# A written-out order of 3,900 entries replaced: other queue orders, one early subtraction moved from GpSimd to VectorE, 13 more products of zeros

## Chip, cores and metric

The kernel runs on one core of a Trainium2 chip. The metric is the device time of one execution in microseconds (us); the time of a kernel is the median of its runs. Three runs of the kernel before gave 851.04, 850.16 and 851.88 us, so their median is 851.04 us.

## What is computed

Attention with two kinds of windows, and behind it two layers of the same shape, all in float32 to the accuracy of float32:

```
scores = q @ k.T / sqrt(64)            # 4 batches, 8 heads, 576 positions, head size 64
mask: heads 0-3: 0 <= i-j < 32;  heads 4-7: 0 <= i-j < 128 and (i-j) % 4 == 0
x = softmax(scores) @ v                # as 2304 tokens x 512
h = x @ w_in;  x = relu(h)**2 @ w_out          # layer 1, 512 -> 2048 -> 512
h = x @ w_in2; out = (h * sigmoid(h)) @ w_out2 # layer 2, same shapes
```

The weights come in as 64-bit floats and are turned into pairs of 32-bit floats on the chip.

## The kernel before

**Products in three parts.** TensorE multiplies in the type fp32r, which keeps fewer bits than float32. So every operand is split in a high part (a cast) and a low part (the subtraction `x - high`, `Kern.sub`, profile line L252), and every product is three matmuls: high x high, high x low, low x high. Casts are at L245 (ScalarE) or L247 (VectorE), and the splits load VectorE most.

**Stages.** Attention works on 32 blocks: half a sequence (288 positions, index h from 0 to 7) times a pair of heads (0 to 3). A block's scores are matmuls at L525. VectorE adds the mask and takes the row minimum (L550). For the first four blocks (h = 0) the method `late_exp` follows: `less` subtracts the row's value from the scores (L683 on VectorE, L686 on GpSimd; one call for each of the two heads of the pair), TensorE transposes the result (L705), ScalarE takes the exponential (L721), TensorE multiplies by the values and a column of ones (L730), VectorE adds a small constant to the row sums (L736) and inverts them (L738), ScalarE or VectorE scales (L746, L743), and TensorE turns the block round (L622). The later blocks do the same in another order (L558 to L622).

Layer 1 begins while attention goes on: `mlp` runs the first three tiles of 256 tokens (L780 to L782 for the first product, L828 to L830 for the second), `mlp2` three tiles of 512 tokens (L928, L982 to L984), and layer 2, `strassen`, three tiles of 768 tokens with seven products in place of eight (L1086, L1171). `weights` loads one piece of the weights as 64-bit numbers (L274), turns it into 32-bit ones (a scaling at L282 on ScalarE or L284 on VectorE, a shift at L293 on VectorE or at L295 on GpSimd, bit operations at L302, L305 and L309), splits it, and writes some of it back to DRAM (L340 and others); `stream` loads such pieces again when a tile needs them (L437).

**Order by hand.** No compiler sets the order. `Planner.order` reads the string `ORDER`, 3,900 entries, and issues the operations in that sequence. An entry is a letter, the number of the operation, and after each `@` the place of a buffer that it takes. The letter names the engine: P TensorE, V VectorE, A ScalarE, G GpSimd, D a transfer, and F a bundle of products of zeros on TensorE (`filler`, L1237), of which the number is the count. Each engine runs its own entries in the order of the string and waits for the operands of the first one that isn't ready. All transfers are issued by one queue, SyncE's (SP), in the same way: a transfer waits until the buffer that it writes is free, or the data that it stores are made, and whatever is behind it waits too. Places count from 0 to about 205 in units of 256 columns of one large on-chip region; two operations that use the same place follow one another.

A GpSimd entry also waits for the last marked VectorE entry before it in the string (`o.turn`, L137, and L1305 to L1308).

**Entries that matter here.** P5 and P36 are the scores of blocks 0 and 1 of h = 0; P67 and P98 those of blocks 2 and 3. V9 and entry 20 are the subtractions for the two heads of block 0 (`less`), V40 and V51 those of block 1, V72 and V83 of block 2, V114 and V103 of block 3. P10 and P21 transpose block 0's two heads, P41 and P52 block 1's. A11, A12, A22 and A23 are block 0's exponentials. P13, P24, P44 and P55 are the products with the values of blocks 0 and 1, P28, P59, P90 and P121 turn blocks 0 to 3 round. D2, D33, D64 and D95 load the queries and keys of the four blocks, D126 and D134 the first two pieces of weights; A127 or V127 scales D126's piece, G128 is its `shift` in GpSimd's form (L295). P1202 is the first product of layer 1. D2283 loads the 256 KB of `w1s` (tile `wc`) that the fourth group of products of step 6 of layer 1's fifth tile needs (P2398). V1753 or A1753 makes the high part of one piece of `w2`, entry 1754 its low part, and D1755 writes the high part and the low part back (`w2s`).

Of the kernel before, what the change touches and what calls it, by code (L numbers as in the profile page):

```python
# [1360 lines left out]
A172@195 V160 A161@100 V1206 D474@26 V166 V167 A1210 A1211@130 P475@3@1@138@2 V489 P1207 V162 P1214@2 V476
A154@168 A477 V491 A492 V480 V478 A479 V173 V493 V168 D261@40 D194@124 V1212 A481 V482 V155 A494 A490 A169@172
P394@1@0@7@0 V397 V495 P387@3 A390@104 A388 V395 P1213 V496 A1215@122 A1216 A1217@118 V483 A485 V404 V396 P398@1
A498 G181 V405 V389 V406 P407@2 V174 V497 V391 V182 V1218 V170 A399 P400@3 A484 A408 P409@2 P486@0 V401 V175
V410 D186@153 A187@5 G188 P499@1 A195@16 V196 A488 P1219 A501 A487 A500 P502@0 D209@187 A210@191 A176@120 V411
V402 V403@183 V183 V412 P413@1 D201@149 V177 P1220@2 V189 A505@146 A503 V504 V190 D507@52 A414 A416 V415
A184@176 V185 D224@108 D418@89 D239@194 D506 A1221@181 A1222 A1223@116 P508@0@3@74@2 V509 A510 V511 A191@28 V524
V513 F7@2 V1224 P1225 V202@202 V417 V522 A512 A514 V197 A523 A525 V526 V198 A527 V528 V515 V192 V529 A530 A531
V516 A517 A518 V203 V199@180 P420@3@0@94@1 V432 V433 V434 V421 V422 P1226@1 P532@2 A534 A1227@161 A1228 V431
P435@0 V204 V423 V424 P425@1 P519@3 A225@199 A436 A262@2 A533 V419 P437@0 A426 P427@1 A520 A521 P535@3 V211 V212  # L1370
V226 V205 V200 V428 A1229@18 V1230 P1231 V438 A206@32 G207 V213 D216@153 A217@95 D231@10 V429 V439 V430@7 V440
A538@132 A536 V537 V227 V218 A214@184 P441@2 A240@78 A232@141 A442 V443 V219 A444@52 V445 V220 V215 P1238@1
A1239@158 A1240 A1241@24 V1242 F5@0 A221@88 G222 D148 D540@127 P541@3@0@149@2 V544 V555 V548 V559 A556 D178
D254@113 D133 D291@80 D446@144 P448@1@2@136@0 V451 A560 V557 A558 A549 V449 V542 V561 A562 V546 P1243 D193 V450
V233 A547 V452 P453@3 A543 A545 A454 V563 V461 V564 P1250@0 V459 V228 V550 V460 V447 V234 V551 V462 P463@3 V552
A229@188 V230 V565 A1251@56 A1252 P455@2 V456 A464 A1253@92 V1254 V457 P553@1 A554 P465@3 V466 V235 D246@73
V458@124 P566@0 V467 P1255 V241 V263 V242 A255@24 V256 A567 P568@0 A468 A236@96 V237 A569 P469@1 A470 V471
A247@12 A571@26 P1232@3 A1233@147 V243 A244@192 A472 A1234 A1235@5 V248 V570 V257 V249 V473 P1262@2 A1263@141
A1264 A1265@108 P1244@0 A1245@37 A1246 A1247@199 D573@15 P574@2@1@20@1 V245 V264 V250 A251@128 V590 V579 V575
A591 V581 V594 A595 V577 V592 V588 A589 D208 D606@7 D284@152 A593 A576 A578 G1248 D276@160 P1256@3 V265 V1515@56  # L1380
P607@2@0@36@0 V610 V621 V1236 V619 V612 P1268@1 P1237 P1249 V1266 V252 V258 A1257@156 A580 A620 V623 A582 V596
A611 A1269@144 V583 V584 V597 V1514@117 V1516@124 V608 P1280@0 A1258 D539 D269@197 V585 P586@2 V1517 V598
V1526@12 A285@0 A622 A1259@72 A1270 A277@110 A1271@146 A624 V625 A266@40 V278 V286 V279 V1260 A613 A609 A1520
A587 V1518@112 P599@1 V614 V1519 V287 V267 V615 P1274@3 A1275@158 P1267 A600 P601@2 A1276 A1523 A270@92 P1261
D633@201 A602 A604@108 D605 D572 D163 D238 V626 V288 A627 A616 V1524 P1286@3 V280 A1287@150 V603 V1272 V1521
P628@2 A629 A1281@4 P617@1 A1288 P1273 A618 A292@140 A1277@147 V271 V272 A281@72 V273 A274@136 V1282 V293
P634@3@1@76@3 V635 V637 V639 A640 V646 V648 V259@132 V650 D299@56 D660@196 D1525 D1522 V260 V282 P630@0
A1289@117 A631@22 V1278 A636 A638 V641 V642 V275 V643 P1292@2 A1293@108 A1294 P1298@3@0@1 A1283@24 A1299@153
A1300 V1527@155 V294 V1290 V295 V1284 P1304@2 V1530@36 A1305@142 P644@3 A645 A1306 A649 P1279 P661@3@2@16@0
V1539@20 P1291 G1528@116 A300@80 A1307@14 V668 V675 A651 V289@144 A647 V652 A676 A1295@157 V653 A654 V664 V666  # L1390
V677 V662 V679 V681 V296@68 P1285 V1538@162 V1296 P655@3 V1540@24 A669 A663 A656 A665 V1529 V297 A667 V670 V1531
D306@92 A678 A682 V671 V301 V1308 V672 V290 A1301@159 A1532 V1302 P1310@2 A1311@148 P1316@3 A1317@150 A1535
A1318 A1319@7 A1312 A1313@82 A680 D223 P1297 V302 V1541 V683 V1542@84 V1543 V1320 P657@3 A307@157 V308 P673@2
A674 V684 A658@4 A685 P1303 V1536 V1550@12 V1314 V303 V309 P1322@2 P1309 D321@112 D632 D314@124 A1323@76
D691@201 A1324 A304@140 V315@162 V305 D329@108 D1537 A1325@58 V322@152 V1533 D1534 P686@3 A687 A1547 V1548 V310
V323 V1551@14 V1326 P1328@2 A1329@78 A1330 A1331@10 P1334@3 A1335@100 A1336 A1337@102 P688@2 A689@16 A1544
A311@116 V316 V317 V318 P1315 P692@3@2@0@2 V695 V710 A696 P1321 V693 A694 V706 V699 A700 V697 A698 A711 A707
V708 A709 V712 A713 P1346@2 V701 V702 V703 P704@3 A705 V1332 V1545 V714 V715 A1347@20 A1348 D722@196 V312
V1562@154 P1327 A716 V319@148 P723@3@2@76@1 V728 A729 V724 A725 V726 A727 V737 V1338 V739 A740 A1349@38 V741
D298 D1546 D690 D1549 D268 D659 D351@92 P1333 V730 V1563@9 V1350 V731 V324 P1340@3 A738 V733 A742 P717@2 A718  # L1400
# [261 lines left out]
```

## Time and profile before

| | us |
|---|---|
| median of 3 runs | 851.04 |
| lowest, highest run | 850.16, 851.88 |
| the profiled execution | 854.73 |
| its span, first to last instruction | 853.0 |

| engine | busy us | share of the span | instructions |
|---|---|---|---|
| TensorE (PE) | 841.8 | 99% | 6012 |
| VectorE (DVE) | 667.9 | 78% | 1786 |
| ScalarE (ACT) | 472.9 | 55% | 1268 |
| GpSimd (POOL) | 35.5 | 4% | 43 |

The profiled execution is a run of its own, 3.7 us above the median of the timed ones; its instructions lie in a span that is 1.7 us shorter than its time. A matmul's end is modelled and matmuls overlap, so that TensorE counts as busy through short waits inside a group of products; the distance from start to start shows those. The page's chain of work that ended last is on TensorE for 90% of the span.

### The profile page before, as it was taken

How to read it: one execution, taken by the hardware profiler on the slowest of the kernel's cores; microseconds unless marked ns; L12 is line 12 of the kernel's file. 1: busy time of each engine (PE TensorE's matmuls, PEld its weight loads, DVE VectorE, ACT ScalarE, POOL GpSimd, SP SyncE). 2: the span in 40 equal slices, each digit the busy share in tenths (PEclk: the TensorE clock that was granted, in tenths of full speed). 3: DMA queues.
4: the chain of work that ended last, by engine and by line, in shares of the span. 5: the costliest groups of instructions: out<-in, count | busy, mean ns of one | idle time of the engine just before them, and what ended most of it. 6: DMA issues, size and time to landing. Idle time of an engine off the chain costs nothing.

```text
span 853.0 us, 16835 instructions
## 1 busy us (share of the span) xinstructions
PE 841.8 (99%) x6012; PEld 797.1 (93%) x6012; DVE 667.9 (78%) x1786; ACT 472.9 (55%) x1268; POOL 35.5 (4%) x43
## 2 busy tenths in 40 slices
PE   8999999999999999999999999999999999999998
PEld 6889999999989989988889899999999999999998
DVE  5999999989987898788899996789812598524782
ACT  3898988767565435333323546675334674346740
POOL 2110000000110000000000000100000000000000
PEclk7999999999999999999999999999999999999999
DMA  7774666778997898976999999886883464965642
GB/s 285 253 259 169 195 231 220 257 246 290 352 318 282 295 337 276 325 289 221 361 317 376 353 325 354 309 281 219 293 316 140 159 237 153 333 207 206 215 155 75
DMA packets 83603, 223.56 MB, mean 262 GB/s; under 512 B 8768, under 2 KB 18240, under 8 KB 83520
## 3 DMA queue, kind: packets, MB, share of 16 engines
q1 hardware_dynamic: 83520, 222.49, 74.4%
q8 instruction: 48, 0.79, 0.4%
q14 instruction: 35, 0.29, 0.1%
HBM read 172.13 MB, written 50.33 MB: 261 GB/s over the span
## 4 chain that ended last, share of the span: by engine, by line
PE 90%; DMA 4%; DVE 4%; ACT 1%; issue 1%; SPq 0%; POOL 0%; DVEq 0%; ACTq 0%
PE y L1086 17%; PE s L928 14%; PE sa L1171 14%; PE y L1171 6%; PE y L982 5%; PE y L983 5%; PE y L984 5%; PE sa L1086 4%; PE s L780 2%; PE ax L525 2%; PE s L782 2%; PE s L781 2%; PE ax L617 1%; PE y L828 1%; PE y L830 1%; PE ax L594 1%
## 5 line engine op out<-in xcount | busy, mean ns | idle before, releaser
L252 DVE TENSOR_TENSOR hl<-gq,hl 128x384 fp32r<-128x384 f32 x164 | 86.4, 562 | 31.9 <-ACT hl L245 31.5
L1086 PE MATMUL y<-xs,ws 128*128 128x384 f32 x552 | 107.0, 334 | 0.0
L245 ACT CAST hl<-gq 128x384 fp32r<-128x384 f32 x168 | 77.4, 512 | 51.1 <-DVE gq L252 20.3
L1086 PEld LDWEIGHTS y<-xs,ws 128*128 128x128 f32 x552 | 96.6, 188 | 0.1
L1062 ACT COPY gq<-y 128x384 f32<-128x384 f32 x92 | 43.1, 480 | 76.6 <-PE y L1086 73.2
L1171 PE MATMUL sa<-hl,wp 128*128 128x384 f32 x432 | 78.6, 334 | 0.0
L928 PE MATMUL s<-x,ws 128*128 128x256 f32 x576 | 76.9, 284 | 0.0
L982 PE MATMUL y<-g,w 128*128 128x512 f32 x192 | 76.2, 397 | 0.0
L1171 PEld LDWEIGHTS sa<-hl,wp 128*128 128x128 f32 x432 | 75.2, 188 | 0.0
L983 PE MATMUL y<-g,w 128*128 128x512 f32 x192 | 75.2, 392 | 0.0
L984 PE MATMUL y<-g,w 128*128 128x512 f32 x192 | 74.8, 390 | 0.0
L558 ACT ACTIVATE ap<-ap,ast 96x128 f32<-96x128 f32 (+3 forms) x168 | 62.3, 372 | 21.5 <-DVE ast L550 18.7
L928 PEld LDWEIGHTS s<-x,ws 128*128 128x128 f32 x576 | 72.8, 191 | 1.3
L944 DVE TENSOR_TENSOR h<-s,h 128x512 f32<-128x512 f32 x96 | 59.6, 621 | 15.4 <-PE s L928 11.2
L1057 DVE TENSOR_TENSOR gq<-y,gq 128x384 f32<-128x384 f32 x46 | 25.0, 553 | 57.4 <-PE y L1086 46.7
L245 ACT CAST g<-r 128x256 fp32r<-128x256 f32 (+1 forms) x94 | 47.7, 508 | 35.1 <-DVE r L964 16.3
L780 PE MATMUL s<-x,w 128*128 128x256 f32 x192 | 56.4, 294 | 0.1
L782 PE MATMUL s<-x,w 128*128 128x256 f32 x192 | 54.5, 284 | 0.1
L781 PE MATMUL s<-x,w 128*128 128x256 f32 x192 | 54.3, 283 | 0.1
L252 DVE TENSOR_TENSOR g<-r,g 128x256 fp32r<-128x256 f32 (+1 forms) x91 | 49.5, 548 | 4.8 <-ACT g L245 4.4
L252 DVE TENSOR_TENSOR gq<-gq 128x384 f32<-128x384 f32 x95 | 50.3, 552 | 3.7 <-ACT gq L1122 3.2
L1171 PE MATMUL sa<-hl,sw 128*128 128x384 f32 x288 | 51.4, 335 | 0.1
(157 smaller groups left out, 1972.4 us busy)
## 6 DMA issues: line engine op xcount, KB each, us to landing
raw<-w SPq DMA_DIRECT2D x64, 512.0 KB, 6.1
ws<-w1x SPq DMA_DIRECT2D x48, 512.0 KB, 6.5
ws<-w2x SPq DMA_DIRECT2D x48, 512.0 KB, 6.3
sw<-w2y SPq DMA_DIRECT2D x48, 512.0 KB, 4.8
wa<-w1s SPq DMA_DIRECT2D x24, 512.0 KB, 5.4
wa<-w2s SPq DMA_DIRECT2D x24, 512.0 KB, 6.5
w1x<-st SPq DMA_DIRECT2D x16, 512.0 KB, 3.7
w2x<-st SPq DMA_DIRECT2D x16, 512.0 KB, 5.9
```

What stands on the lines that cost most here:

```text
L245: self.nc.scalar.copy(out=out, in_=in_)
L252: self.eng[eng].tensor_tensor(out=out, in0=a, in1=b, op=ALU.subtract)
L558: es.append(self.op({"ACT": c_act(nk) + 0.185}, lambda e, i=i, n=n, c=c, p=p, st=st: nc.scalar.activation(out=p.tile[:n, c], in_=p.tile[:n ...
L780: nc.tensor.matmul(o, wh.tile[:, s], xh, start=(kk == 0), stop=False)
L781: nc.tensor.matmul(o, wh.tile[:, s], xl, start=False, stop=False)
L782: nc.tensor.matmul(o, wl.tile[:, s], xh, start=False, stop=(kk == KC - 1))
L928: nc.tensor.matmul(bank.tile[:, o:o + 256], wp, xp, start=i == 0, stop=last, skip_group_check=True)
L982: nc.tensor.matmul(o, wh.tile[:, s], gh.tile, start=c == 0, stop=False)
L983: nc.tensor.matmul(o, wh.tile[:, s], gl.tile, start=False, stop=False)
L984: nc.tensor.matmul(o, wl.tile[:, s], gh.tile, start=False, stop=(c == NF - 1))
L1086: nc.tensor.matmul(o, w[part == 2].tile[:, kk * P:kk * P + P], x[b][part == 1].tile[:, kk * half:kk * half + half], start=new and not kk a ...
L1171: nc.tensor.matmul(o, u.tile[:, c * P:c * P + P], v.tile, start=new and not q and not part, stop=q == nf - 1 and part == 2, skip_group_che ...
```

## The change

The diff replaces `ORDER` as a whole: 245 lines go, 246 come, and no other line changes. Both strings hold the same 3,892 operations and eight bundles of zeros, each operation once. What differs:

- The order on each engine. Of TensorE's 746 entries 297 have another rank among TensorE's, by at most 14; of VectorE's some 1,400 of 1,560, by at most 41; of ScalarE's some 930 of 1,035, by at most 31; of the 516 transfers 469, by at most 21.
- The engine of 141 operations, nearly all of them casts, copies and scalings that change between VectorE and ScalarE. Entry 20, the subtraction of block 0's second head, goes from GpSimd (L686) to VectorE (L683). Entry 127 goes from VectorE to ScalarE, entry 1754 from VectorE to GpSimd, and 1753 from ScalarE to VectorE.
- The buffers' places (851 operations).
- The bundles of zeros: 10, 9, 4, 7, 8, 6, 7, 5 (56 in all) become 14, 11, 7, 7, 12, 8, 5, 5 (69).

The beginning of the string, and the lines around D2283, 1754 and D1755, before and after:

```diff
@@ -1348,250 +1348,251 @@
 APART = ()
 V_LAG = 3
 ORDER = """
-V1 F10@0 D2@72 P5@22@0 G0 V17 V6 V19 V18 D33@67 V7 P36@112@1 V8 V9 V37 V48 F9@1 P10@0 G20 P21@1 A11 V39 A22 V50
-V49 V51 P52@2 A53 A12 A23 A54 D64@195 P67@58@2 D126@173 V127@55 G128 V38 V40 P41@2 A43 A42 D34@100 V80 D96@90
-D3@43 V4 F4@0 D134@145 A135@9 D95@165 V71 V68 V129 V70 P13@0 V14 V35 V79 V15 P24@1 V25 V81 V69 V26 V82 A16@155
-A27 P44@3 V45 V46 A47@77 V72 P98@72@3 V100 V101 V112 V113 P55@2 V56 V57 D65@64 F7@0 P73@0 V102 A58 A74 V66 V99
-V83 V111 V110 V114 P28@1 A31@48 A29@44 V32 V136 V30 P59@2 A62 P84@3 A85 P75@0 V76 V103 A60 V61 V97 V77 V63
-P115@3 A116 P86@1 V87 V78@170 D141@122 A142@82 P104@3 A105 D366@15 F8@3 V88 A89 P90@3 A91@60 A93@64 V137 V130
-A131@68 G132 V138 V143 A139@164 G140 D149@107 A150@88 V92 P106@0 V107 V94 P117@2 V118 V108 V119 V109@182 V120
-P368@3@1@1@0 V369 V378 V379 F6@0 D392@133 D156@36 A157@31 A3890 D164@111 V380 P381@2 A382 V371 V370 V144 V367
...
-V2385 P2381@2 D2288@60 D2237 D1747 P2343 D2283@14 D1766@201 V1767@32 V1768 D2284@39 P2395@0 P2396@1 A1760 V2355
-V1754 A2392@196 V2393 V2402 V2403 V2404@110 V2246@108 V2387@10 A2247@44 V2249@34 V2248 V1770 D2289@39 A2388@201
-P2429 P2430 A1843@16 V1844 V1845 V1779@60 V1780 V1787 P2431 A1819@42 G1820 D1755 A1826@18 V1827 V1821 V2500
...
+V1 F14@1 D2@166 P5@140@3 G0 V8 V7 V6 V18 V9 D33@79 P36@33@1 V17 D126@89 A127@157 G128 F11@3 P10@3 A11 V19 V20
+P21@0 A22 A12 A23 V37 V50 V48 V39 V38 V40 D64@151 P67@186@2 P41@2 A42 D3@99 V4 P13@1 V49 V51 P52@0 A53 A54 A43
+D34@0 D134@29 A135@104 V68 V79 V70 V129 V80 V35 V82 V14 V15 V69 F7@3 P24@0 V71 V72 V81 P44@3 V45 V25 V26 V46
+A16@130 V27 P55@2 V56 V83 V57 A47@20 A58 V136 D95@174 P98@201@0 V111 V102 V112 V113 V110 D65@119 V66 V101 V100
+V114 P73@0 P28@1 A29@44 A74 A31@48 V30 F7@3 P59@2 A60 V61 P84@3 A85 A62 V32 P75@0 V76 V99 P115@3 A116 P86@1 V77
+A78@71 V103 P104@3 A105 V87 V63 V88 A89 F12@2 D179@7 D96@110 V97 D141@146 A142@170 P90@3 A91@60 A93@64 V130
+A131@68 P106@0 V137 V138 A139@164 D156@23 A3890 A157@34 V143 V92 V107 P117@2 V118 V94 V108 V109@120 V119 V120
+D366@79 P368@3@1@1@3 V379 V380 V378 G132 F8@0 G140 V369 V371 V370 P121@1 A122 V144 A180@192 A124 V367 V158
+D149@153 D164@18 D261@40 A150@11 P381@0 A382 P372@3 A373 V145 A146@84 A165@36 V123 P1202@2 V151 V159 A1203@146
...
+V2370@94 A2371@42 V1185 P1199@0 V2374@12 A2375@197 V2383 V2384 V1753@120 G1754 D1170 D1766@20 D2287@78 D1729
+P2397@1 P2360 D2236@96 D2238@28 D1201 V2387@26 V2376 V2391@32 D2237 D1755 A2240@48 D2283@24 P2398@0 P2373 D2239
...
 """
```

## Rows read from the trace of the kernel before

**Rows 1.** Windows: us, then busy us (instructions) of each engine, clock, DMA share, GB/s

```profile
0.00:27.28 27.28, 22.78 (x188) 18.25 (x189) 16.23 (x100) 11.88 (x40) 5.04 (x15) 0.81 0.83 298
27.28:100.00 72.72, 71.55 (x726) 66.58 (x726) 71.52 (x288) 64.53 (x212) 7.22 (x7) 1.00 0.59 202
100.00:140.00 40.00, 39.93 (x389) 38.11 (x387) 38.62 (x141) 35.45 (x123) 0.74 (x1) 1.00 0.71 245
140.00:380.00 240.00, 238.68 (x1995) 219.28 (x1992) 208.19 (x632) 135.54 (x449) 8.82 (x8) 1.00 0.84 294
380.00:849.40 469.40, 468.77 (x2726) 454.88 (x2724) 333.30 (x629) 224.98 (x446) 13.71 (x13) 1.00 0.73 256
```

**Rows 2.** Timeline of TensorE, first 10 us: start us, us, line, operation, tiles

```profile
0.98 2.31 PE L1237 MATMUL fill<-warm 128*128 128x256 bf16 x10 [0.98 <-DVE warm L1229]
3.75 2.66 PE L525 MATMUL y<-w 64*96 64x96 f32 x24 [0.46 <-DMA w<-qkv]
6.35 1.16 PE L1237 MATMUL fill<-warm 128*128 128x256 bf16 x9
7.35 0.44 PE L705 MATMUL ax<-ident,ap 96*128 96x96 f32 x3
8.86 0.30 PE L705 MATMUL ax<-ident,ap 96*128 96x96 f32 x1 [1.06 <-POOL ap L686]
9.71 1.06 PE L705 MATMUL ax<-ident,ap 96*128 96x96 f32 x5 [0.56 <-POOL ap L686]
```

**Rows 3.** Waits of TensorE, the longest in total: us, times, longest

```profile
PE ax L705 <- POOL ap L686: 1.6, 2, 1.1
```

**Rows 4.** Windows around the stretch at the lower clock, columns as in rows 1

```profile
6.28:9.70 3.42, 1.81 (x15) 1.21 (x13) 3.42 (x22) 1.53 (x2) 2.39 (x4) 1.00 1.02 376
9.70:19.93 10.23, 10.16 (x74) 8.57 (x75) 5.65 (x44) 4.76 (x20) 0.59 (x1) 0.50 0.76 302
19.93:40.00 20.07, 18.67 (x193) 16.58 (x191) 18.80 (x79) 16.30 (x52) 2.51 (x2) 1.00 0.76 256
```

**Rows 5.** Timeline of VectorE, 5 to 11 us

```profile
5.42 0.25 DVE L550 CUSTOM_DVE_ANT_0 ap<-y,mask 96x96 f32<-96x96 f32 x1 [4.49 <-PE y L525]
...
6.62 0.58 DVE L683 TENSOR_TENSOR ap<-ap,ast 96x96 f32<-96x96 f32 x2
...
8.12 0.60 DVE L683 TENSOR_TENSOR ap<-ap,ast 96x96 f32<-96x96 f32 x2
...
9.21 1.52 DVE L683 TENSOR_TENSOR ap<-ap,ast 96x96 f32<-96x96 f32 x2
```

**Rows 6.** Timeline of GpSimd, 7 to 11 us

```profile
7.31 2.35 POOL L686 TENSOR_SCALAR ap<-ap,ast 96x96 f32<-96x96 f32 x3 [4.84 <-DVE ap L683]
9.64 0.65 POOL L295 TENSOR_SCALAR raw<-raw 128x512 f32<-128x512 f32 x1
```

**Rows 7.** Groups of VectorE's instructions by form: count, busy us, mean ns

```profile
L284 DVE TENSOR_SCALAR cv<-raw 128x512 f32<-128x512 f32 x23 | 9.7, 420 | 2.3 <-DMA raw<-w 2.3
L247 DVE CAST st<-cv 128x512 fp32r<-128x512 f32 x10 | 4.2, 420 | 0.5 <-issue 0.4
```

**Rows 8.** Around a load near 385 us: SP, landing, entry 1754, TensorE, GpSimd's splits, write-back

```profile
364.35 0.37 SPq L437 DMA_DIRECT2D wc<-w1s  x1
...
wc<-w1s SPq DMA_DIRECT2D x1, 256.0 KB, 7.6
...
384.07 0.69 DVE L252 TENSOR_TENSOR st<-cv,st 128x512 fp32r<-128x512 f32 x1
...
386.39 0.88 PE L928 MATMUL s<-x,wc 128*128 128x256 f32 x6
...
L252 POOL TENSOR_TENSOR st<-st 128x512 fp32r<-128x512 f32 x2 | 2.6, 1294 | 33.3 <-DMA ws<-w2x 33.3
...
405.82 0.43 SPq L340 DMA_DIRECT2D w2s<-st  x1
```

More of the change, by code (lines that the diff above doesn't have):

```diff
@@ L1361 @@
[L1361 to L1400, printed above, removed]
@@ new lines @@
+V1041 P2122 A2137@108 V2138 V1039 A2133@47 V2134 A1000 A1009 D1670@93 D2069@21 D1696@6 D2071@106 A1029 A1013
+A1011 A1027 A1042 V1014 V1015 V1032 A1033 V1034 V1035 V1671@26 V1017 V1001 V1002 A1697@14 V1045 V1672 A1040
+V1036 A1004 A1046 P2140@3 P2141@0 P2135 P2139 A2144@49 V1016 V2145 V1691 D961 D2072@28 D1509 D2079@98 A1003
+V1673 V1674 V1678@108 P1005@3 A1007 P1018@0 P1037@1 D1507 D2075@10 D930 V1680@92 D2070@54 D1055@196 D1669
+P2142@2 A1044 V1047 V1020 D2074@76 A1019 A1006 P1021@3 D2073@44 V1048 D992 V1049 P1050@0 A1038 V1022@58 V2146
@@ new lines @@
+V1095 V2216 V2217@73 V1105 V1106 A1107 D1085 D2033 P2173 P2186 P2190 D1714@97 P1108@2 D1684 D2034@49 D2035
+D1722@108 D1703 V1709 D1710 D2258@33 V1715@13 V1716 V2206 V1096 V2042@85 V2045@57 P1097@1 P2203 P2207 D1687
+D2261@9 V2048@31 V1115 V1130 D2262@112 V1126 D2260@45 D2266@22 A2218@40 V2219 A1098 A1116 A1127 A1118 A2046@116
+V1119 V2221@37 A1120 V1717 V1109 V1718 A2038@64 V2039 V2051@75 V1128 A2040@80 A2222@71 A2052@88 V1719@27
+A2036@104 A1131 A1129 V1723@68 V2041 V1724 V2037 P1110@3 V2053 D1740@96 V1121 V1122 V2223 A1123 P2220 P2224
@@ new lines @@
+D2472@108 P2428 P2429 P2515@1 P2430 P2516@0 P2517@3 A2432@14 P2431 V1821 V1822 V1826@18 V1827 V1828 V1790
+V2503@4 D2471@88 V1829 A1823@203 V2510@97 D1791 V2519 V2520 V1832@60 G1824 V2521 D2477@128 V1834@198 V2522
+V2527@57 V1833 V2436@122 P2531@0 P2532@1 A2535@32 V2523@30 V2536 D1866@72 D2474@84 A1867@0 V1868 V2434@90
+A2524@23 A2438@2 A2504@124 P2533@2 P2534@3 P2548@1 V1835 A1839 V2505 P2506 P2507 D1792@92 V1793@8 P2508
+A2511@117 V2512 P2509 P2513 V2537 V1869 D1773 V1846 V2538 V2539 V2540@88 D2476@40 V2525 P2526 D2481@4 D1849@100
@@ new lines @@
+D2478@96 V2544@27 D1890@64 D1873@10 D2475@80 D2437 D2433 D2484@32 V1840 D1841 A1836 V1837 A2528@68 V1870
+V1850@124 V1851 V1852 V2529 D2480@20 D2483@14 D2439 D2479@29 D1838 V1794 A2541@116 P2549@3 P2550@2 P2551@0
+A2552@172 V2553 V2542 P2530 V2554 V2555 V2556 V2561@80 V2557@110 V1795 V1853 V1856@164 V1796 V1857 V1858@198
+V1859 P2565@1 A2569@82 P2566@2 P2567@1 D2482@168 V2570 V2571 V1874@70 V2572 A2558@174 V2559 V1875 A1863 A2545@60
+V2546 A1860 P2568@0 P2543 P2547 D2487@68 V1876 V1877 V1861 A2562@40 V1864 P2582@3 P2583@2 D2485@120 P2584@1
@@ new lines @@
+D1897@92 A1898@102 G1899 A1891@100 V1892 D1865 P2560 V1882@116 V2573 V1880@72 V1881 V2574@2 A2575@32 V1893 V1900
+A1884 A2586@23 V2587 V2563 V2588 V2589 V2578@182 V1871@178 G1872 P2585@3 V2590 V2595@126 V1901 D2486@108
+V2591@80 A2592@24 V1883 V2576 V1894 A2579@120 V2580 V1904@28 P2599@1 A2603@168 A1797@4 D2435 D1862 D1914@86
+D2491@57 D2488@96 D2489@196 P2564 P2600@2 P2601@1 P2602@0 V1906@108 V2604 V2605 V2606 V1798 A1847@197 V1885
+V1905 V2607 V2612@91 V1848 V1907 V2608@128 P2577 D2490@10 P2616@3 A2620@189 D2492@82 P2617@2 D2440@172 D2441
@@ new lines @@
+D2713@56 P2991 P2995 V2998 A3037@72 A3029@60 V3048 V3030 P3002@0@3 A3041@42 A3045@119 D2644@66 D3087@161
+D3086@104 D2645 A2648@75 D3088@186 P3005 P3008 P3011 P3014 P3017 P3020 V2962 V3056 D3092@100 D2646@10 D2647
+G2649 V2650 V2960 A3033@86 V2996 A2651@112 V2652 V3034 V2660 V3046 A3053@151 V3054 P3023 V3026 P3134 P3136
+D3093@122 V3038 V3042 V2655 P3031 P3035 P3039 P3043 P3047 V3024 A3137@61 A2658@55 A2661@22 V2662 A2653@87 V2654
+P3138@0 D2963 D3090@4 D3089@127 D3098@136 D2961 D3027 A2656@16 V2657 A3135@52 A3057@172 V2659 V2663 A2664@28
@@ new lines @@
+V3072 A3477@71 A3469@126 V3470 D3486@4 V3075 P3455 P3459 P3463 A3465@151 A3076@34 V3080 A3078@74 V3466 V3474
+D3488@62 P3534 P3467 P3471 P3475 V3077 V3446 A3073@87 V3074 V3083 V3478 A3081@40 V3079 V3082 P3479 P3536@2
+A3533@16 A3535@19 P3538 P3540 A3539 P3542 V3444 V3541 P3544 P3546 V3537 V3547 P3549@1 A3543@28 A3545@31 P3551
+D3383 D3502@150 D3491@95 D3496@123 D3494@136 D3492@80 G3084@46 V3085 P3553 A3554 A3555 D3505@186 D3495@69
+D3499@11 P3556 A3552 V3557 P3558 P3560 A3480@2 A3559@52 A3660@112 A3482 P3562 P3565@0 P3567 A3561@62 A3568
@@ L1595 @@
+P3823 P3826 V3814 D3815 P3829 P3832 P3835 A3859@86 A3855@118 A3871@176 V3872 V3852 A3847@101 V3780 D3781 V3856
+V3866 V3816 V3848 P3838 P3841 P3849 P3853 P3857 A3867@75 V3868 V3844 V3860 P3861 V3864 P3865 P3869 V3876 P3873
+P3877 P3880 P3881 P3882 V3842 D3843 P3883 P3884 P3885 P3886 P3887 A3878@91 A3888 D3845 D3817 D3879 V3778 D3779
+D3889
 """
```

388 lines of the change are left out of this document (195 added, 193 removed).

## The prediction

> **What bounds the kernel now.** I read the windows first, by stage, to see which engine has no room where [rows 1]. After 140 us TensorE is busy for 238.68 of 240 us and then for 468.77 of 469.4, while VectorE has over 30 and 130 us to spare: there a table can win little. From 27.28 to 140 us TensorE is nearly full too, but VectorE stands idle for only 72.72 - 71.52 = 1.2 us and 40 - 38.62 = 1.4 us: VectorE has no room there. It makes the operands, and TensorE's rows are long because a matmul that waits inside a group is counted as busy. So between 27 and 140 us work that VectorE has to do, and the moment at which it gets going, set the time. In the first 27.28 us no engine is full: VectorE is idle for 11.05 us, TensorE for 4.5, and its mean clock is 0.81.
>
> Next I read that start closely. TensorE's timeline [rows 2] shows what it waits for: ten products of zeros, 0.46 us for the first load, the scores, nine products of zeros, three transposes, and then twice for GpSimd's subtraction, 1.06 and 0.56 us. The list of waits sums these to 1.6 us [rows 3]. GpSimd needs 2.35 us for its three pieces [rows 6], VectorE 0.58 to 0.60 us for a subtraction group of the same size [rows 5]. The windows around it give the clock [rows 4]: 1.00 (2.4 GHz) from 6.28 to 9.70, then 0.50 (1.2 GHz) from 9.70 to 19.93, and 1.00 from there. It fell right after TensorE's two waits for GpSimd. In the 10.23 us at 0.50 TensorE is busy for 10.16 and VectorE for only 5.65: here TensorE at half speed holds up everyone, and the block chains of attention run late by it.
>
> **The change, part by part.** The sum is made on the profiled execution, which took 854.73 us, 3.7 above the median of 851.04; I carry differences over to the median.
>
> *More zeros ahead of the scores, ten to fourteen.* Ten took 2.31 us, so four more are 0.92; the wait of 0.46 for the load takes half of that [rows 2]. Bounds 0 (the clock rises sooner) and +0.5; I take **+0.3**.
>
> *Entry 20 on VectorE.* TensorE's 1.6 us of waiting for GpSimd go [rows 3]. VectorE does 0.6 us more, in a start in which it idles for 11.05 [rows 1, 5]; but next to it GpSimd's L295 of 0.65 us, now entry G128, may run [rows 6]. While that ran in the kernel before, two subtractions took 1.52 us in place of 0.6 [rows 5], 0.9 more; I charge half of it, 0.4. That is **-1.2**, bounds -1.6 and -0.7. The two additional zeros of the second bundle (1.16/9 = 0.13 us each [rows 2]) lie in what is left of TensorE's wait for the subtraction; uncovered they would cost 0.3. A GpSimd entry waits for the VectorE entry marked ahead of it, but behind G128 on GpSimd stands only work on weights, which layer 1 needs well after the first blocks.
>
> *The clock.* With the waits closed and zeros in the gaps (14, 11, 7, 7 and 12 where there were 10, 9, 4, 7 and 8) I expect that it stays at 1.00. The work of the 10.23 us stretch [rows 4] then takes at least VectorE's own 5.65 us, which gives a bound of -4.6; the other bound is 0, if the chains through ScalarE and VectorE set the time anyway. TensorE's 10.16 busy us at full clock would be 5.1, so that VectorE and the hand-overs from engine to engine decide. Adding a fifth for these makes 6.8 of the 5.65, and half a microsecond for a landing that is late makes 7.3: **-2.9**. Both additions are guesses between the bounds. This is the largest and least certain term.
>
> *The other additional zeros*, thirteen less the six above: seven more, at 0.13 us each [rows 2], are 0.9 if nothing hides them. They stand where TensorE waits for the exponentials or the subtractions; I take **+0.2**, bounds 0 and +0.9.
>
> The start is then 0.3 - 1.2 - 2.9 + 0.2 = -3.6 us. It is passed on whole, since up to 140 us the engine that bounds is VectorE, which then begins its full stretch that much sooner [rows 1], and the tables keep their sequence of stages.
>
> *Work that changes engine.* Counted by the entries ahead of TensorE's same marks, up to 140 us 13 operations leave VectorE and 9 come, entry 20 among them. At 0.42 us for a cast or scaling of 128x512 [rows 7] that is 13 x 0.42 = 5.5 out and 8 x 0.42 + 0.6 = 4.0 in, -1.5; as several are narrower I take **-1.0**, bounds -1.9 and 0. ScalarE takes them over; it is idle for 72.72 - 64.53 = 8.2 us there and 4.5 in the next window [rows 1], which hides 2 to 3 us of new work. Without that cover, the 2 to 3 us would come back whole.
>
> *The transfers.* 469 of 516 have another rank, all on SP's queue. The DMA share is 0.59 to 0.84 after the start [rows 1], so that it isn't the rate but the order of issue that could make one late. Setting old landing times against the new order, I find that nearly all keep some microseconds of lead. The tightest is D2283 (below). For the rest **+0.3**, bounds 0 and, if D2283 is late, +7.1.
>
> *After 140 us.* Other ranks, other buffers, 141 changes of engine: TensorE is full and VectorE has room [rows 1], so **0**. The cover is VectorE's 32 idle us of 240; a late operand would show as a wait of TensorE.
>
> Sum: -3.6 - 1.0 + 0.3 = -4.3 us, 851.04 - 4.3 = **846.7**.
>
> **The rivals.** *A, the forecast:* 846.7.
>
> *B, the clock falls all the same.* There are still waits for the first exponentials and landings, and 0.3 - 1.2 + 0.2 - 1.0 + 0.3 = -1.4 gives 849.6. For it: nothing in the trace says which idle brought it down; against it: 1.06 and 0.56 us are the only waits between the full and the half clock [rows 2, 4]. The Trainium skill, page "TensorE: Matmul & The Clock Gate", section "HAM oscillation — how this bites in real kernels", shows the clock falling in long waits for a transfer between groups of matmuls; by that the two short waits here would not be the cause, and closing them would return nothing of the clock, as in this rival. The trace of before disagrees so far, with a clock of 0.50 right behind waits of 1.06 and 0.56 us.
>
> *C, the start's gain is given back before 140 us.* If layer 1's and the blocks' inputs are set by landings and not by VectorE, the whole start waits for them later: -1.0 + 0.3 gives 850.3. For it: the DMA share of 0.83 in the first 27 us [rows 1]; against it: VectorE idles for only 1.2 us behind it.
>
> *D, slower: one late load.* In the new order D2283 stands on SP behind D1755, a write-back that waits for entry 1754, and 1754 is now on GpSimd, where such a split takes 1.29 us and not 0.69 [rows 8]. Before, the load was issued at 364.35, landed 7.6 us later and was used at 386.39; the write-back came at 405.82. If 1754 ended only when it did before, about 384.8 (384.07 + 0.69), the issue at some 385.2 and 7.6 us give a landing at 392.8, and the products at 386.39 wait for 6.4 us; with the 0.6 that GpSimd is slower, 7.0. At +7.1, which the -4.3 does not cover, it is 853.8. The point that decides is whether 1754 ends ahead of about 386.4 - 7.6 = 378 us by the old clock. The new table puts it 47 entries sooner; at 851 us for 3,900 entries that is an estimated 10 us, so that it would end near 375, and I hold it for harmless, with 3 us to spare.
>
> *E, more:* the clock at its bound of -4.6, the whole 1.6, and -1.9 of VectorE's work: 0.3 - 1.6 - 4.6 + 0.2 - 1.9 = -7.6, 843.4.
>
> **How the numbers follow.** A .53, B .14, C .12, D .11, E .10. What a measurement of this kernel tells from no change is about 0.2%, 1.7 us, as its runs lie from 850.16 to 851.88; so faster is below 849.3, slower above 852.7. A counts .50 faster and .03 the same; B .04 faster, .09 the same, .01 slower; C .01, .09, .02; D .01 the same, .10 slower; E is faster. Together faster .65, same .22, slower .13. The range takes in A with its bounds, B and C and most of E: 843.0 to 851.5. D and the rest of E and C lie outside.
>
> **What would show it.** Right: the clock row from 9.7 to 20 us at 1.00; no wait of TensorE for GpSimd's L686, which has gone from the timeline; VectorE's idle time ahead of the first layer 1 product down from 11 to about 7 us, and that product about 3.6 us sooner; VectorE's busy time up to 140 us down by about 1 us; no wait of TensorE for `wc` near 380 us; the stretch from 380 to the end as long as before. Wrong: a clock still at 0.50 anywhere in the first 20 us (B); the first layer 1 product 4 us sooner but the mark at 140 us where it was, with VectorE or TensorE idle behind DMA in between (C); TensorE waiting some 7 us for `wc` (D); or new waits of over 1 us behind 140 us, where I put nothing.

## The result, and the profile after

The changed kernel took 843.15 us in the median of four runs (842.81 to 843.33); the kernel before took 851.46 in four (850.16 to 852.28). The ratio is 0.9903, 95% interval 0.9886 to 0.992: 1% faster, 8.3 us. The forecast was 846.7 in a range from 843.0 to 851.5, so that the sign was right and the time lies at the range's lower end. The profiled execution of after took 842.81 us, its span is 841.0; that of before took 854.73, span 853.0. So the two traces differ by 12.0 us and the medians by 8.3, and the traces of before and after can't be subtracted as they stand.

The windows of after, at the edges of [rows 1], but that the last one runs to the end of the span where [rows 1] stops 3.6 us short of it (us, then busy us and instructions of TensorE, its weight loads, VectorE, ScalarE and GpSimd, then clock, DMA share, GB/s):

```profile
0.00:27.28 27.28, 24.65 (x268) 21.29 (x269) 21.95 (x127) 17.00 (x53) 4.81 (x13) 1.00 0.92 329
27.28:100.00 72.72, 71.83 (x743) 67.47 (x743) 71.70 (x286) 68.44 (x233) 5.84 (x6) 1.00 0.68 239
100.00:140.00 40.00, 39.96 (x379) 38.46 (x379) 39.20 (x129) 32.70 (x109) 0.74 (x1) 1.00 0.58 190
140.00:380.00 240.00, 239.92 (x1979) 219.79 (x1975) 211.50 (x634) 132.17 (x435) 10.35 (x10) 1.00 0.86 301
380.00:841.00 461.00, 457.52 (x2669) 446.05 (x2667) 326.13 (x617) 219.21 (x437) 19.58 (x14) 1.00 0.72 254
```

In the first 27 us the clock is 1.00 and VectorE idles for 5.33 us in place of 11.05. Behind that VectorE is still nearly full up to 140 us. From 140 to 380 us TensorE is idle for 0.08 us in 240, where it was idle for 1.32.

TensorE's timeline at the start, beside [rows 2], shows the new order of the first blocks:

```profile
0.98 3.04 PE L1237 MATMUL fill<-warm 128*128 128x256 bf16 x14 [0.98 <-DVE warm L1229]
3.95 1.46 PE L525 MATMUL y<-w 64*96 64x96 f32 x24
5.34 1.37 PE L1237 MATMUL fill<-warm 128*128 128x256 bf16 x11
6.82 0.94 PE L705 MATMUL ax<-ident,ap 96*128 96x96 f32 x6
8.00 0.74 PE L525 MATMUL y<-w 64*72 64x72 f32 x16 [0.24 <-DMA w<-qkv]
...
24.66 0.36 PE L780 MATMUL s<-x,w 128*128 128x256 f32 x1
```

Both heads of block 0 are transposed in one go (six at 6.82), no wait for GpSimd is left, and the first product of layer 1 (P1202) comes at 24.66 us, against 30.84 in the trace of before. The first scores took 1.46 us in place of 2.66: in this execution the clock rose ahead of them. (The clock column of the windows doesn't tell, as it shows 1.00 from the start in either trace; the products of zeros do: here 3.04/14 = 0.22 us each ahead of the scores and 1.37/11 = 0.12 behind, in before 2.31/10 = 0.23 ahead of them and 1.16/9 = 0.13 behind.)

VectorE, ScalarE and GpSimd at the start of after, one fence each (the subtractions beside [rows 5]; what ScalarE did first; GpSimd's L295):

```profile
5.76 0.58 DVE L683 TENSOR_TENSOR ap<-ap,ast 96x96 f32<-96x96 f32 x2
6.65 0.58 DVE L683 TENSOR_TENSOR ap<-ap,ast 96x96 f32<-96x96 f32 x2
8.15 0.94 DVE L683 TENSOR_TENSOR ap<-ap,ast 96x96 f32<-96x96 f32 x2
```

```profile
0.73 1.28 ACT L282 ACT_TABLE_LOAD   x1 [0.73 <-PEq L1654]
7.22 0.68 ACT L282 ACTIVATE cv<-raw 128x512 f32<-128x512 f32 x1 [5.21 <-DMA raw<-w]
7.80 0.80 ACT L721 ACTIVATE ap<-ax 96x96 f32<-96x96 f32 x4
```

```profile
7.98 0.66 POOL L295 TENSOR_SCALAR raw<-raw 128x512 f32<-128x512 f32 x1 [5.51 <-ACT cv L282]
```

One thing here stood in no term of the sum: ScalarE's first instruction is now the scaling A127, and its table is loaded at 0.73 us, while nothing is there to do (in the trace of before at 6.96, ahead of the first exponential). What the forecast had charged is there too: the pair of subtractions that runs beside GpSimd's L295 took 0.94 us where the others took 0.58, 0.36 more, and the term for entry 20 had 0.4 for it.

The load of rival D, beside [rows 8]: SP's timeline, the landing, GpSimd's timeline and TensorE's:

```profile
366.70 0.64 SPq L340 DMA_DIRECT2D w2s<-st  x1
367.39 0.53 SPq L437 DMA_DIRECT2D wc<-w1s  x1
```

```profile
wc<-w1s SPq DMA_DIRECT2D x1, 256.0 KB, 6.5
```

```profile
362.80 1.61 POOL L252 TENSOR_TENSOR st<-cv,st 128x512 fp32r<-128x512 f32 x1 [18.75 <-issue]
```

```profile
376.22 0.88 PE L928 MATMUL s<-x,wc 128*128 128x256 f32 x6
```

The split on GpSimd ends at 364.41, SP issues the write-back 2.3 us later and the load right behind it. The load lands after 6.5 us, at 373.9, and the products come at 376.22, without a wait for `wc`.

### The profile page after: what moved, and what is told of

Same layout as the page of the kernel before. It is cut to its first block, busy times and chain, and to the rows that moved or that the text cites. A ratio compares the mean times of both kernels' runs of the same rounds, so it can differ in the third digit from the quotient of the medians.

```text
span 841.0 us, 16837 instructions
## 1 busy us (share of the span) xinstructions
PE 833.9 (99%) x6025; PEld 793.1 (94%) x6025; DVE 670.5 (80%) x1789; ACT 469.5 (56%) x1263; POOL 41.3 (5%) x44
## 4 chain that ended last, share of the span: by engine, by line
PE 95%; DVE 2%; ACT 1%; DMA 1%; SPq 0%; issue 0%; DVEq 0%; ACTq 0%
PE y L1086 17%; PE sa L1171 15%; PE s L928 14%; PE y L1171 6%; PE y L982 5%; PE y L983 5%; PE y L984 5%; PE sa L1086 4%; PE s L780 3%; PE ax L525 2%; PE s L781 2%; PE s L782 2%; PE y L828 2%; PE ax L617 2%; PE y L830 2%; PE y L829 2%
## 5 line engine op out<-in xcount | busy, mean ns | idle before, releaser
L558 ACT ACTIVATE ap<-ap,ast 72x72 f32<-72x72 f32 (+3 forms) x168 | 62.3, 373 | 16.2 <-DVE ast L550 13.6
L780 PE MATMUL s<-x,w 128*128 128x256 f32 x192 | 56.5, 294 | 0.0
L1171 PE MATMUL y<-hl,sw 128*128 128x384 f32 x288 | 51.4, 334 | 0.0
```

Source lines behind the costliest of these rows:

```text
L558: es.append(self.op({"ACT": c_act(nk) + 0.185}, lambda e, i=i, n=n, c=c, p=p, st=st: nc.scalar.activation(out=p.tile[:n, c], in_=p.tile[:n ...
L780: nc.tensor.matmul(o, wh.tile[:, s], xh, start=(kk == 0), stop=False)
L1171: nc.tensor.matmul(o, u.tile[:, c * P:c * P + P], v.tile, start=new and not q and not part, stop=q == nf - 1 and part == 2, skip_group_che ...
```

## The experiments

Two theories. The forecast's (**W** in the first four texts below, **S** in the others): the start is the gain, by the waits for GpSimd and the clock, and what follows passes it on. Its rival (**T**, then **O**): zeros and subtraction do little, and the orders of the queues, further on above all, make the gain.

The ratios below are those on record, against runs of before taken beside, with their 95% interval. They aren't quotients of the two medians (for the zeros alone 1.0033, where the medians give 856.86/850.41 = 1.0076), so that the readings go by medians, and where it matters by the runs that kept the clock.

**The kernel before again.** No edit.

> The kernel before once more, nothing changed, for a second trace. The profiled execution of before took 854.73 us, 3.3 above the median of its timed runs (851.46). Theory W (waits and clock: TensorE's two waits for GpSimd bring the clock down in every execution, and the start costs the 8 us): 851.5 in the median, and the clock at 0.50 for about 10 us after 9.7 us here too. Theory T (the low stretch of the one trace was chance, and the table's later part is what gains): 851.5 too, but with a clock of 1.00, or a much shorter low stretch, in this trace.

Measured: 850.58 in the median of ten, ratio to the runs of before beside it 1.0003 (0.9961 to 1.0045). The profiled execution took 857.35 us. The clock around the start:

```profile
9.64:20.00 10.36, 10.27 (x75) 8.33 (x75) 6.19 (x49) 4.95 (x20) 0.58 (x1) 0.53 0.82 321
20.00:30.00 10.00, 9.33 (x66) 8.26 (x66) 5.73 (x20) 5.61 (x18) 0.54 (x1) 0.50 0.74 254
30.00:31.50 1.50, 1.50 (x14) 1.25 (x12) 1.03 (x5) 1.11 (x3) 1.50 (x2) 0.50 0.00 0
```

Here it was low for more than 20 us, over twice as long as in [rows 4]. Each run is listed with its mean clock, and that settles what the profile of before could not say. Of 103 runs of the kernel before that were taken beside these experiments 64 have a mean clock of 0.997 or more, with a median of 850.2 us; 19 have 0.99 to 0.997 and 853.8; 18 have 0.98 to 0.99 and 858.9 (two more lie under 0.95 and fit neither; a 104th took 3980.8 us and is left out). All 103 together: 850.8. So by the mean clocks it falls in 37 of 103 executions and costs 853.8 - 850.2 = 3.6 or 858.9 - 850.2 = 8.7 us there; the execution that I had summed up was one of the 19. The median run has no such stretch, and a kernel that keeps the clock gains 0.6 us in the median. Both theories were half right: the fall is real and no matter of one trace, but it isn't in most executions.

**The zeros alone.**

```diff
-V1 F10@0 D2@72 P5@22@0
+V1 F14@0 D2@72 P5@22@0
...
```
The other bundles likewise: 9 to 11, 4 to 7, 7, 8 to 12, 6 to 8, 7 to 5, 5.

> The kernel before with the counts of the new table in its eight bundles of zeros (14, 11, 7, 7, 12, 8, 5, 5), nothing else. Theory W: four more zeros ahead of the scores keep TensorE busy until the load has landed, so that the clock rises before the scores and not behind them (they took 2.66 us in the kernel before and 1.46 after), -1 us; the waits for GpSimd stay, but whether the clock falls behind them is open: 850.5 if it falls, 847 to 848 if it stays. Theory T: seven zeros more on TensorE in places where they are in the way, 851.5 to 852.5.

Measured: 856.86, 12 runs from 851.35 to 860.87; ratio 1.0033 (0.9995 to 1.0071). Four runs kept the clock, with 851.7 in the median, 1.5 over the 850.2 of before at that clock. In eight of 12 it fell. Theory W's 847 to 850.5 isn't there. T's price is right for the runs that kept the clock, but not for the median, and more zeros did not protect the clock.

**Entry 20 alone.**

```diff
-V8 V9 V37 V48 F9@1 P10@0 G20 P21@1
+V8 V9 V37 V48 F9@1 P10@0 V20 P21@1
```

> The kernel before with entry 20 on VectorE and not on GpSimd, zeros as they were. Theory W: TensorE's 1.6 us of waits for GpSimd go, the clock doesn't fall at 9.7 us, -1.2 - 2.9 us: 847 to 848. If the clock falls all the same (other waits stand there): 850.3. Theory T: 851 to 851.5, since VectorE is what bounds the stretch up to 140 us and has one piece of work more.

Measured: 849.46 (847.49 to 851.12), ratio 0.9967 (0.9937 to 0.9997). All 12 runs kept the clock at 0.999 or more, as W had it, and yet only 1.4 us are gained of the 4.1 that the forecast had for this entry and the clock. The waits of TensorE and two windows (of its profiled execution, 848.59 us):

```profile
PE ax L705 <- DVE ap L683: 1.0, 2, 0.6
```

```profile
6.16:9.46 3.30, 2.27 (x20) 1.62 (x18) 3.30 (x22) 1.78 (x3) 0.02 (x1) 1.00 1.00 374
9.46:20.00 10.54, 9.40 (x117) 7.93 (x116) 9.48 (x65) 8.28 (x32) 0.65 (x1) 1.00 1.03 409
```

The 1.6 us of waiting for GpSimd [rows 3] have become 1.0 of waiting for VectorE, which is busy for all of the 3.30 us. At the same clock the entry gives 850.2 - 849.5 = 0.7 us, which is not clear of the scatter: the 64 runs of before at that clock lie from 847.1 to 852.3.

**Both.** The two edits above together.

> The kernel before with both, entry 20 on VectorE and the new counts of zeros; the queue orders, the engines of the other operations and the transfers as before. Theory W: the clock rises ahead of the scores and stays, 0.3 - 1.2 - 1.2 - 2.9 + 0.2 = -4.8: 846.7, and the first product of layer 1 at 26 us in place of 30.84. Theory T: these two parts are worth less than 2 us together, 849.5 to 851.5, and the other 6 us and more come from the orders.

Measured: 851.45, ratio 1.0013 (0.9983 to 1.0044); eight runs kept the clock, with 850.45, four did not (854.2 to 857.6). Theory T's 849.5 to 851.5. At that clock the zeros cost 850.45 - 849.46 = 1.0 us against entry 20 alone, within the scatter, and four of 12 runs fell where none had.

**The changed kernel again.** No edit.

> The changed kernel once more, nothing edited, to see how its runs scatter beside the kernel before: that one took 847.5 to 852.3 us in the 24 of 34 runs with a mean clock of 0.997 or more, and 852.2 to 860.4 in the ten with a lower one. Both theories: 843.2 in the median. Theory S (start: the gain comes from the first 25 us): no run with a clock below 0.998, 842.5 to 844. If some runs here too have a lower clock, 5 to 9 us more in these, the change doesn't protect the clock and the median's gain is of another origin.

Measured: 843.41 (843.18 to 843.58), ratio 0.9883 (0.9839 to 0.9927), the clock at 1.0 in all four. Against the 850.8 of the 103 runs of before this is 7.4 us; the 8.3 of the first section rest on four runs of before. The kernel has lost the scatter as well: its eight runs so far lie within 0.8 us, where the 64 of before with the clock up scatter by 5. In this profiled execution the scores took 2.67 us again:

```profile
4.08 2.67 PE L525 MATMUL y<-w 64*96 64x96 f32 x24
```

and P1202 came at 25.05, 0.4 us later than in the first trace; the end was 0.4 later too (span 841.4). So the moment at which the clock rises differs from one execution to the next, and between these two it is worth 0.4 us. (The Trainium skill, page "TensorE: Matmul & The Clock Gate", section "What's actually happening", says that the moment of the rise varies between runs of one kernel, because what the chip watches isn't started by the kernel; these two traces agree: 1.46 and 2.67 us for the same scores behind the same 14 zeros.)

**The changed kernel with the old counts of zeros.**

```diff
-V1 F14@1 D2@166 P5@140@3
+V1 F10@1 D2@166 P5@140@3
...
```

> The changed kernel with the counts of zeros of before (10, 9, 4, 7, 8, 6, 7, 5), all else as changed. Theory S: the thirteen zeros make the clock rise ahead of the scores and hold it: without them the scores take 2.66 us again in place of 1.46 and the clock falls in some runs: 844.5 to 846 in the median, single runs over 848. Theory O (orders: the gain is made by the queue orders, at equal clock zeros only cost time, as 849.8 to 851.5 us with them added to the kernel before): 842 to 843.2, and the clock stays up since nothing waits for GpSimd.

Measured: 843.15 (843.06 to 844.1), ratio 0.9884 (0.9845 to 0.9923), the clock at 1.0 in six of six. The thirteen zeros are worth nothing in the new order, neither way: 843.15 without them, 843.15 and 843.41 with them. Theory S's 844.5 to 846 is out.

**New start, old rest.** The new table up to P1202, behind it what is left of the old one; two lines at the seam:

```diff
-V145 A146@84 A180@78 V123 P1202@2 A1203@34 A124 A1204
+V145 A146@84 A165@36 V123 P1202@2 D392@133 A1203@5 A1204
```

> The new table up to and with the first product of layer 1 (P1202, 25 us), and behind it the operations that are left in the order of the old table, on the old engines. Theory S: the start is the gain, since VectorE bounds what follows and passes it on: 843 to 845. Theory O: the traces at full clock (before with entry 20 on VectorE, against the changed kernel) differ by 1.4 us at P1202 and by 5.7 at the end; so this makes 847 to 849, with the clock at 1.00 in every run.

Measured: 854.02 (eleven runs from 853.09 to 854.89; a twelfth took 4128.56), ratio 1.0024 (0.9998 to 1.005): slower than both expectations. P1202 comes at 24.61, as hoped, but then the seam costs:

```profile
33.51 1.49 PE L525 MATMUL ax<-blk 64*96 64x96 f32 x12 [4.74 <-DMA blk<-qkv]
```

SP had stood still from 17.24 to 29.50 us, since the next load waits for a buffer place that the new head keeps in use longer. That is a fault of the splice and says nothing on the theories.

**New table to P1364 (140 us), old rest.**

```diff
-P719@2 A720@84 A1568 V745 P1364@3 A1365@114
+D1570 V743 V744 V337@160 P1364@3 D298 D690 D268 V332 V746
```

> The new table up to P1364 (140 us in the kernel before), and behind it what is left in the old order. Theory S: as in the run with the new table up to 25 us, 843 to 845, since nothing more is gained behind the start. Theory O: the same two traces differ by 3.5 us near 140 us, so 845 to 846, some 2.5 us below the run with the new start alone, and 2 above the changed kernel.

Measured: 849.93, ratio 0.9963 (0.9935 to 0.9991), far from 845 to 846. Up to the seam it is as fast as the changed kernel: at the 97th matmul of L780 126.63 us, against 126.42 there and 129.92 with entry 20 alone. Behind it TensorE waits, once, for VectorE:

```profile
PE ax L594 <- DVE r L804: 2.5, 1, 2.5
```

Four VectorE operations that the old order had done by then and the new one had not are now at the head of VectorE's queue, and VectorE is busy for 13.74 of the 14 us from 126 to 140; the clock falls behind the wait (0.93 in that window). So part of the lead at a mark is work that the new order has put off, and it is kept only with an order behind that has a place for it.

**The first splice with other places.** As the new start with the old rest, D474 at place 52 in place of 26, and twelve more places moved.

> The run with the new table up to P1202 again, with other buffer places behind the seam: there D474 waited for a place that came free only at 29.5 us, and TensorE for its landing, 4.7 us. Theory S (start): 843 to 845. Theory O (orders further on): TensorE at P1202 near 24.7 us, 1.3 ahead of the 26.0 of the kernel before with entry 20 on VectorE (849.46 in the median), and this lead kept to the end: 847.5 to 849.

Measured: 855.78, ratio 1.0025 (0.9995 to 1.0056). The lead at P1202 (24.78 us) is kept to about 60 us, where TensorE again waits for a block:

```profile
PE ax L525 <- DMA blk<-qkv: 3.9, 1, 3.9
```

and the clock falls behind that (0.64 from 60 to 70 us). Spoilt in the same way.

**New table to P2086 (219 us), old rest.**

```diff
-V1654@4 V1655 A1487@67 V1488 P2086@3 P2087@2
+A2027@60 V2028 V1655 V2019 P2086@3 D2059@18 D2058@40
```

> The new table up to P2086 (the first product of the 512-token tiles, 219 us in the kernel before), what is left in the old order. Attention is over there and VectorE has idle time on both sides of the seam. Theory S: 843 to 845. Theory O with the gain between 25 and 219 us: in the traces the changed kernel is 4.5 us ahead there and 5.7 at the end, so 844.4 to 845.2. If the seam costs again as the one at 140 us did (2.5 us of waiting for VectorE), 847, and that says that the new order owes VectorE's work at the mark and pays it later.

Measured: 851.16, ratio 0.9982 (0.9947 to 1.0017). P2086 comes at 209.80 us (209.75 in the changed kernel), 4.4 us ahead of the run with entry 20 alone. Behind it the lead is lost to waits for transfers and to the clock that falls with them (0.91 from 260 to 280 us):

```profile
PE s L928 <- DMA ws<-w1x: 2.5, 3, 1.8
```

Neither expectation: it was VectorE that I had expected to pay, and it was SP's queue. What the later part of the order is worth isn't told by it.

**Entry 20 on VectorE and early.**

```diff
-V8 V9 V37 V48 F9@1 P10@0 G20 P21@1
+V8 V9 V20 V37 V48 F9@1 P10@0 P21@1
```

> The kernel before with entry 20 on VectorE and right behind V9, ahead of V37 and V48, as the new table has it. With entry 20 behind V48 TensorE waited twice for VectorE's subtractions (0.42 and 0.61 us), and block 1's scores began at 9.46 us; in the changed kernel it waits for neither and they begin at 8.0 to 8.9. Theory S: the first 25 us are what counts: -1 and what follows from it, 848 to 848.5. Theory O: VectorE's pieces only change places, block 1's come later by what block 0's come sooner: 849 to 849.8, no clear difference from 849.46.

Measured: 850.02, ratio 0.996 (0.9929 to 0.9992), 849.6 in the ten runs with the clock up: theory O, no difference from 849.46. In the profiled execution TensorE's wait for VectorE has only moved (block 1's subtraction is late now), and the clock fell once more, with nothing of GpSimd in front of it:

```profile
6.92 0.94 PE L705 MATMUL ax<-ident,ap 96*128 96x96 f32 x6 [0.41 <-DVE ap L683]
8.82 0.47 PE L705 MATMUL ax<-ident,ap 96*128 96x96 f32 x3 [0.97 <-DVE ap L683]
```

```profile
9.20:20.00 10.80, 10.21 (x94) 8.66 (x92) 6.90 (x53) 5.95 (x25) 0.66 (x1) 0.68 0.94 348
```

**Old start, new rest.** The splice the other way round. Of the new head only A124, D261 and A165 are still to be done at the seam; five places are moved, and D418 is put at 157.

```diff
-V8 V9 V37 V48 F9@1 P10@0 G20 P21@1
+V8 V9 V37 V48 F9@1 P10@0 V20 P21@1
...
-V145 A146@84 A180@78 V123 P1202@2 A1203@34 A124 A1204
+V145 A146@84 A180@78 V123 P1202@2 A124 D261@40 A165@80 V151 V159 A1203@146
```

> The other way round: the old table with entry 20 on VectorE up to P1202 (26 us at full clock), and behind it what is left in the new order, on the new engines, with five buffer places other than the table's and D418 at a place that is free. Only three operations of the new head are still to be done at the seam. Theory S: the start is the gain, so it is lost: 848.5 to 850. Theory O: only the 1.4 us up to P1202 are lost, the 4.3 us behind it are kept: 849.46 - 4.3 = 845.2, 844.5 to 846.5. If it is slower than 850, the seam itself costs, as at the other three, and the two theories aren't told apart by it.

Measured: **845.11** (844.58 to 845.99), ratio 0.9918 (0.9891 to 0.9946), the clock at 0.999 or more in 12 of 12. Theory O's 845.2. So with the start of the old table, its zeros and entry 20 on VectorE, the new order behind P1202, engines and places included, gives 849.46 - 845.11 = 4.35 us; the new start, with all that hangs on it, gives the other 845.11 - 843.41 = 1.7.

Where these lie is read from windows between the same marks of TensorE, in three profiled executions at full clock: P1202, the 97th matmul of L780, the 151st of L828, the end. First with entry 20 alone, then the old start with the new rest, then the changed kernel:

```profile
0.00:26.03 26.03, 21.82 (x229) 17.90 (x229) 19.41 (x121) 13.86 (x44) 4.80 (x13) 1.00 0.85 322
26.03:129.92 103.89, 102.47 (x1019) 96.07 (x1018) 101.33 (x392) 93.04 (x314) 5.88 (x6) 1.00 0.63 216
129.92:190.16 60.24, 59.47 (x564) 57.23 (x563) 55.96 (x175) 43.20 (x142) 0.74 (x1) 1.00 0.75 254
190.16:846.70 656.54, 653.05 (x4208) 622.06 (x4206) 491.09 (x1104) 322.56 (x772) 21.75 (x20) 1.00 0.77 270
```

```profile
0.00:25.92 25.92, 21.16 (x228) 17.18 (x229) 19.41 (x121) 13.83 (x44) 4.79 (x13) 1.00 0.87 315
25.92:128.37 102.45, 101.06 (x1016) 95.35 (x1016) 100.43 (x386) 93.65 (x314) 6.57 (x7) 1.00 0.65 220
128.37:187.63 59.26, 59.26 (x564) 57.31 (x563) 56.38 (x179) 44.61 (x146) 0.00 (x0) 1.00 0.72 260
187.63:843.30 655.67, 651.83 (x4208) 621.85 (x4206) 494.45 (x1107) 317.06 (x761) 30.22 (x24) 1.00 0.77 271
```

```profile
0.00:24.66 24.66, 22.03 (x244) 18.67 (x244) 19.33 (x120) 14.43 (x47) 4.81 (x13) 1.00 0.91 324
24.66:126.42 101.76, 100.83 (x1017) 95.32 (x1016) 100.20 (x386) 93.34 (x313) 6.58 (x7) 1.00 0.64 224
126.42:185.68 59.26, 59.26 (x565) 57.29 (x563) 56.40 (x179) 44.66 (x146) 0.00 (x0) 1.00 0.73 260
185.68:841.00 655.32, 651.75 (x4208) 621.78 (x4206) 494.55 (x1107) 317.09 (x761) 29.93 (x24) 1.00 0.77 271
```

Read down a column of lengths: from the first fence to the third the stages shrink by 1.4, 2.1, 1.0 and 1.2 us, 5.7 in all, and none by much. (Entry 20's profiled execution was 0.9 us faster than its median, so that the first two fences differ by 3.4 us where the medians differ by 4.35.) In the second stage VectorE is the one with no room: its work falls from 101.33 to 100.20 and its idle time from 103.89 - 101.33 = 2.6 to 1.6. In the third TensorE's 0.8 us of idle time go, nearly all of it one wait:

```profile
PE ax L594 <- DVE ap L578: 0.7, 1, 0.7
```

In the fourth, three quarters of the kernel, VectorE does 3.5 us more, which costs nothing there, and the stage is 1.2 us shorter.

One trace of the old order is not all of them. In the five others with the old rest (two of the kernel before, the zeros alone, both edits, entry 20 early) the second stage takes 103.4 to 103.9 us, the third 60.8 in the first of before, but 59.4 to 59.7 in the other four, and the fourth 657.0 to 659.3. In the two further traces of the changed kernel, again and with the old zeros, the second takes 101.7 and 102.0, the third 59.3, the fourth 655.3. So the second stage and the fourth are shorter in every one of them, by 1.4 to 2.2 and by 1.2 to 4.0 us; most of the third stage's 1.0 belongs to executions in which that one wait occurs.

Most of the second stage's gain, and over half of the fourth's, is in short delays that no list of waits shows. In the second stage, with entry 20 alone, 101 distances from the start of a matmul to the start of the next are 0.05 to 0.3 us longer than usual (the median for the same line and form), 10.3 us together; in the changed kernel they are 86, 8.6 us together. In the fourth they are 110 with 10.9 us, and 102 with 10.2.

## Why the prediction was right, and where it was not

**The sign and the bounds: right.** VectorE, busy for 101.33 of 103.89 us, has no room in the stretch up to 130 us, an order that feeds TensorE sooner is passed on, and D2283 is harmless. The deciding point, 378 us by the old clock, is 376.22 - 7.6 = 368.6 in the trace of after; 1754 ended at 364.41, 4.2 us ahead of it, where I had estimated 3.

**The clock, -2.9: the step that failed.** "The work of the 10.23 us stretch" was taken as a part of every execution. It was a part of the profiled one; 64 of 103 runs have none that lowers the mean clock under 0.997. In the median the whole clock is worth 850.8 - 850.2 = 0.6 us. The warning stood in the table: the profiled execution took 3.7 us more than the median, about what one such stretch costs (3.6). I wrote that difference down and carried the terms over all the same. For an execution in which the clock does fall for some 10 us, 2.9 is near the 3.6 that it costs; it was the share of such executions that I had wrong. The mechanism itself was right in part: with entry 20 on VectorE behind V48 and the old zeros the clock fell in none of 24 runs (two kernels), and in the changed kernel in none of the eight. But it isn't GpSimd's wait alone that brings it down: it fell in two of 12 with the entry early, and in four of 12 with the added zeros.

**Entry 20, -1.2: too large.** TensorE's 1.6 us of waiting for GpSimd went, as forecast, but 1.0 came back as waiting for VectorE, which I had called free because it idles for 11 us in the whole start. In the 3.4 us that matter it had no idle time at all, as [rows 4] show (3.42 of 3.42). The entry was worth 0.7 us at the same clock, in the old order and within the scatter.

**The zeros, +0.3 and +0.2:** about nothing in the new order; in the old order they cost 1.0 to 1.5 us at the same clock, the lower figure within the scatter, and did not hold the clock. The rising of the clock ahead of the scores, which I had as a bound, came in the first trace of after and not in the second.

**VectorE's work, -1.0: right** (101.33 to 100.20 between 26 and 130 us). By the two strings 136 operations change engine, and not 141; the term doesn't rest on that count.

**What had no term.** The start's own order (1.4 us to P1202 at full clock), VectorE's idle time behind it (1.0 us from 26 to 130), and the stages behind 130 us (1.0 and 1.2 us), where I put 0 because TensorE was busy for 238.68 of 240 us. The 1.32 us that are missing there stood in the list of waits, right behind the line of [rows 3], and I passed over it:

```profile
PE ax L594 <- DVE ap L578: 1.3, 1, 1.3
```

This wait (at 183 us) is gone in the changed kernel; the second trace of the kernel before hasn't got it either. The rest no list shows: the busy share hides short waits inside groups of matmuls, and mostly these are what the new order takes out in the second stage and the fourth. Two errors of opposite sign, then: the clock 2.9 - 0.6 = 2.3 us too large, and the orders, by the medians, 4.35 + 1.7 = 6.05 us where the sum had 1.0 - 0.3 = 0.7. That the result lies by rival E's 843.4 isn't E's doing, since its largest term was the clock; and that it lies inside the range, 0.15 us above its lower bound, is luck, as that bound was drawn to take in most of E.

**The pass-on "whole"** was right for the old and new tables, each by itself: in the traces with the old table in which P1202 came 1.5, 2.8, 4.8, 6.2 and 9.5 us later than with entry 20 alone, the end came 1.1, 2.1, 6.3, 7.9 and 8.9 us later. The splices show how far it goes: all four with the new head lost their lead to the first transfer or VectorE entry for which the rest had no room, and only the old head with the new rest kept what it had.

**Still open:** how the 1.7 us of the new start divide among the earlier table load, the order of the subtractions and the loads; entry 20 early was tried alone and gave nothing, the table load wasn't tried. How the 4.35 us behind P1202 divide between the sequence of the queues, the changes of engine and the places isn't shown either, nor why the runs of the kernel before scatter by 5 us at one clock while those of the changed one don't, nor why added zeros went with more falls of the clock. No trace of the kernel before itself at the full clock was taken; entry 20 alone stands for it in the stages.

## What to carry to other kernels

Before a stall of one trace becomes a term of a sum, set the profiled execution against the median of the runs: if it is off by as much as the stall, look at the mean clock of several runs first. An engine's idle time counts only where the new work falls; take it from a window as narrow as the work. Read the list of waits to its end before a stage gets a 0. And an order that is tuned as a whole can win most where no line of the page shows it, in many waits of tenths of a microsecond, and its head can't be taken over alone: it leaves undone what its tail makes room for.
